# Even and odd rows kept apart in the block transforms, with other work between their steps

## Chip, cores and metric

The kernel runs on one core of a Trainium2 chip. The metric is the device time of one execution in microseconds (us). Before the change it was 556.54 us, the median of 3 runs from 553.25 to 558.03. An execution that takes over 1.5% longer than the fastest one of its kernel counts as slow.

## The reference

```python
def reference(A_q, A_k, A_v, A_shift_k, A_ssm_k, A_ssm_D, B_x, B_w1, B_w3, B_w2, c, w_mod):
    def _A_ref(q, k, v, shift_k, ssm_k, ssm_D):          # S = 2048 rows, D = 576 columns
        k_shift = ...            # causal convolution of k with 4 taps per column
        kv = k_shift * v
        # causal convolution over the 2048 rows, column by column, written with FFTs of length 2*S
        y_f = rfft(pad(kv)) * rfft(pad(ssm_k))
        y = irfft(y_f)[:S].astype(bfloat16) + kv * ssm_D
        return q * y
    x = A_q
    sa, ca, ga, sb, cb, gb = (silu(c) @ w_mod).reshape(...)
    h = layernorm(x) * (1 + ca) + sa
    x = x + ga * _A_ref(h, A_k, A_v, A_shift_k, A_ssm_k, A_ssm_D)
    h = layernorm(x) * (1 + cb) + sb
    return x + gb * ((silu(h @ B_w1) * (h @ B_w3)) @ B_w2)      # F = 4608 hidden columns
```

(Inputs are bfloat16.)

## The kernel before

The 2048 rows are cut into 8 blocks of 256. Each block of the signal `kv` and of the filter is transformed by matmuls with a matrix of sines and cosines. Products of the spectra X and V of different blocks are summed up in `z` by VectorE, and one inverse transform gives a block of the result. Two blocks make a row block of 512 rows for the feed-forward part; row block 3 has no convolution beside it. While TensorE works through the feed-forward part of row block r (the up projections, `stream`, then the down projection, `down`), the convolution of the next two blocks is fed in between in small steps: a step that is a generator yields its estimated VectorE time, and a negative yield means "let that much other work come first".

```python
def forward(self, basis, rhs, dst):                  # one transform: 4 outputs
    for e in range(2):
        for cs in range(2):
            ps = self.ps()                           # one of four accumulators
            for cc in range(2):                      # row parity: both are summed in PSUM
                for h in range(2):
                    nc.tensor.matmul(ps[:, h, 0:H], basis[:, cc, cs, e, :],
                                     rhs[:, cc, h * H:(h + 1) * H],
                                     start=(cc == 0), stop=(cc == 1))
            nc.scalar.copy(dst(e, cs)..., ps[:, :, 0:H])
            yield 0.4

def ln_scales(self, ssum, ssq, name):                # six small GpSimd operations on 128x2
    e.tensor_single_scalar(mean[:], ssum[:], -1.0 / D, op=ALU.mult)      # "l1m"
    e.tensor_scalar(var[:], ssq[:], 1.0 / D, EPS, op0=ALU.mult, op1=ALU.add)
    e.tensor_mul(rstd[:], mean[:], mean[:])
    e.tensor_sub(var[:], var[:], rstd[:])
    e.tensor_tensor(rstd[:], var[:], self.neghalf[:, 0:n], op=ALU.pow)
    e.tensor_mul(nmr[:], mean[:], rstd[:])                               # "l1n"

def gate_rows(self, s):                              # waits for l1n, in ScalarE's queue
    for i in range(2):
        self.nc.scalar.activation(hg[:, i, :], x1[:, i, :], ACT.Identity, bias=..., scale=...)

def conv(self, s0):                                  # blocks s0 and s1 = s0 + 1; cut
    def filters():
        yield from self.k_rows(s0);  yield -4.0
        yield from self.w_spectrum(s0);  yield -3.0
        yield from self.v_block(s0)
        yield from self.k_rows(s1);  yield -4.0
        yield from self.w_spectrum(s1)
    yield from self.mix(filters(), old())            # old(): products with kept spectra
    self.gate_stats(s0)
    yield from self.kv_rows(s0)                      # shift convolution
    yield from self.v_block(s1)
    self.gate_rows(s0)
    yield from self.x_spectrum(s0)                   # the signal's transform
    yield from self.pair(X0, self.V[s0], s0)
    ...
    yield from self.gate(s1)
    yield from self.pair(self.X[s1], V0, s1)
    yield from self.outcome(s1)                      # inverse, residual, second layernorm, transposes
```

(Cuts are marked by dots.) In `stream`, ScalarE empties an accumulator twice (`sg` = silu of the gate, `u` = copy of the up projection) and VectorE multiplies the two into `h`. `hg` are a block's rows after the first layernorm, `h2row` those after the second; the six operations of `ln_scales` make the scale and offset for either one (`l1...` and `l2...`). PSUM holds the accumulators `ps` that the matmuls write.

## Time and profile before

| | before |
|---|---|
| median of 4 runs | 555.5 us |
| span of the trace | 551.6 us |
| TensorE / VectorE / ScalarE / GpSimd busy | 519.7 / 317.1 / 302.2 / 47.0 us |
| TensorE idle | 31.9 us |

In the lines of the profile PE is TensorE, PEld its weight loads, DVE VectorE, ACT ScalarE, POOL GpSimd and SP the engine that issues transfers; `L414` is line 414 of that kernel; the granted clock is the share of TensorE's full clock that it was given. The reading of this profile stands in the prediction below. One line that the prediction did not look at became important. It is from the groups of instructions of the kernel before: engine, operation, output and inputs, count, busy us, mean ns, then the idle time before the group.

```profile
L414 POOL TENSOR_SCALAR l1m<-l1s 128x2 f32<-128x2 f32 x7 | 7.6, 1086 | 243.9 <-ACT junk L399 243.9
```

The timeline of GpSimd shows the longest of these seven and the statistics operation after it; start, duration, engine, line:

```profile
357.97 3.38 POOL L414 TENSOR_SCALAR l1m<-l1s 128x2 f32<-128x2 f32 x1 [63.30 <-ACT junk L399]
361.44 0.20 POOL L416 TENSOR_TENSOR l1r<-l1m 128x2 f32<-128x2 f32 x1
```

An operation on 128 x 2 elements normally takes about 0.20 us (0.72 us for the power) in this trace, as in the second line. This one took 3.38 us, and the mean of its group is 1.09 us. Little hung on it: ScalarE waited 0.5 us in all for such results at `hg` in blocks 1 to 7.

### The profile page before, as it was taken

What the parts mean: (1) busy time and instruction counts of PE and PEld (TensorE: products, weight loads), DVE (VectorE), ACT (ScalarE), POOL (GpSimd) and SP (SyncE); (2) the same over time, 40 slices, a digit from 0 to 9 for tenths busy, and PEclk for the clock granted to TensorE, in tenths of its full rate; (3) what the DMA queues carried; (4) which work ended last, traced back from release to release, by engine and by line L of the source; (5) the groups of instructions that cost most, each with busy time, mean ns of one, the idle gap of its engine ahead of it and who ended that gap; (6) DMA issues with size and microseconds to landing.
All of it is one profiled execution on the core that took longest, in us unless ns stands there. A gap on an engine that the chain in (4) does not pass through costs nothing.

```text
span 551.6 us, 9038 instructions
## 1 busy us (share of the span) xinstructions
PE 519.7 (94%) x3495; PEld 303.8 (55%) x3495; DVE 317.1 (57%) x489; ACT 302.2 (55%) x637; POOL 47.0 (9%) x111
## 2 busy tenths in 40 slices
PE   6978899998989999999998999989999999999996
PEld 3655665455757534434576644344478744444775
DVE  8989366796980286693983259979442111222011
ACT  6567697859532457749815165675956054554100
POOL 4321100203020000001001000030201000000000
PEclk9979999999998999999999999999999999999999
DMA  8945789998995686975997679654264545442452
GB/s 264 337 120 172 226 276 312 350 359 283 312 337 169 201 284 217 320 239 177 298 324 231 176 241 354 201 165 157 87 177 125 152 159 162 150 122 73 106 152 86
DMA packets 103214, 119.29 MB, mean 216 GB/s; under 512 B 5187, under 2 KB 93316, under 8 KB 103172
## 3 DMA queue, kind: packets, MB, share of 16 engines
q1 hardware_dynamic: 103150, 118.72, 68.4%
q8 instruction: 27, 0.44, 0.3%
q14 instruction: 15, 0.12, 0.1%
q10 hardware_dynamic: 22, 0.01, 0.0%
HBM read 104.84 MB, written 13.86 MB: 215 GB/s over the span
## 4 chain that ended last, share of the span: by engine, by line
PE 54%; DVE 18%; ACT 12%; DMA 9%; issue 4%; POOL 3%; SPq 1%; DVEq 0%; ACTq 0%
PE ps L821 25%; PE ps L875 20%; DMA wst<-in_B_w_dram 5%; DVE p L378 4%; ACT junk L399 4%; PE ps L828 4%; DVE z L380 3%; PE ps L286 3%; DMA X<-Xd 2%; DVE h L838 2%; ACT h2row L511 2%; DVE kvt L305 1%; DVE kv L306 1%; ACT sg L835 1%; ACT hg L454 1%
## 5 line engine op out<-in xcount | busy, mean ns | idle before, releaser
L821 PE MATMUL ps<-h2T,wst 128*128 128x512 bf16 (+1 forms) x1344 | 268.0, 349 | 6.1 <-DMA wst<-in_B_w_dram 4.9
L821 PEld LDWEIGHTS <-wst 128*128 128x128 bf16 x1344 | 125.8, 98 | 131.1 <-issue 20.8
L835 ACT ACTIVATE sg<-ps 128x512 bf16<-128x512 f32 (+1 forms) x168 | 91.7, 546 | 148.6 <-PE ps L828 98.3
L875 PE MATMUL ps<-w2t,h 128*128 128x288 bf16 x1152 | 145.3, 288 | 2.4 <-DMA w2t<-in_B_w_dram 2.4
L875 PEld LDWEIGHTS <-h 128*128 128x128 bf16 x1152 | 113.0, 98 | 32.3 <-DMA w2t<-in_B_w_dram 3.0
L838 DVE TENSOR_TENSOR h<-sg,u 128x512 bf16<-128x512 bf16 (+1 forms) x168 | 63.8, 384 | 106.6 <-ACT u L837 106.5
L837 ACT CAST u<-ps 128x512 bf16<-128x512 f32 (+1 forms) x168 | 89.2, 531 | 0.8 <-DVE h L838 0.8
L886 DVE TENSOR_TENSOR og<-ps,gbrow 128x288 bf16<-128x288 f32 x32 | 13.1, 451 | 83.5 <-PE ps L875 83.5
L378 DVE TENSOR_TENSOR p<-X,V 128x3456 bf16<-128x3456 bf16 x28 | 54.7, 1953 | 5.1 <-DMA X<-Xd 4.9
L380 DVE TENSOR_TENSOR z<-z,p 128x3456 bf16<-128x3456 bf16 x28 | 54.7, 1952 | 0.1
L399 ACT ACTIVATE junk<-x 128x576 bf16<-128x576 bf16 x58 | 40.2, 692 | 13.8 <-DVE x L499 13.3
L828 PE MATMUL ps<-h2T,wst 64*128 64x512 bf16 (+1 forms) x336 | 45.2, 350 | 0.8 <-ACT X L289 0.5
L414 POOL TENSOR_SCALAR l1m<-l1s 128x2 f32<-128x2 f32 x7 | 7.6, 1086 | 243.9 <-ACT junk L399 243.9
L828 PEld LDWEIGHTS <-wst 64*128 64x128 bf16 x336 | 10.6, 94 | 30.4 <-issue 27.4
L286 PE MATMUL ps<-kv,Fb 128*128 128x288 bf16 x128 | 19.0, 286 | 4.1 <-ACT u L837 2.3
L686 ACT CAST y<-ps 128x576 bf16<-128x576 f32 x14 | 8.9, 644 | 22.1 <-PE ps L483 22.1
L511 ACT ACTIVATE h2row<-x,l2n,l2r 128x576 bf16<-128x576 bf16 (+1 forms) x28 | 16.2, 676 | 8.0 <-POOL l2n L419 8.0
L305 DVE TENSOR_TENSOR kvt<-kh,shk 128x1152 bf16<-128x1152 bf16 x24 | 18.1, 753 | 1.8 <-DMA kh<-in_A_k_dram 1.7
L289 ACT CAST W<-ps 128x576 bf16<-128x576 f32 x32 | 18.9, 667 | 0.2 <-PE ps L286 0.2
L289 ACT CAST X<-ps 128x576 bf16<-128x576 f32 x32 | 18.9, 663 | 0.0
L286 PE MATMUL ps<-kT,Fk 128*128 128x288 bf16 x128 | 18.9, 296 | 0.0
L286 PEld LDWEIGHTS <-Fb 128*128 128x128 bf16 x128 | 11.8, 97 | 12.2 <-issue 6.7
(119 smaller groups left out, 327.3 us busy)
## 6 DMA issues: line engine op xcount, KB each, us to landing
wst<-in_B_w_dram SPq DMA_DIRECT2D x80, 512.0 KB, 5.5
w2t<-in_B_w_dram SPq DMA_DIRECT2D x72, 288.0 KB, 3.1
X<-Xd SPq DMA_DIRECT2D x12, 864.0 KB, 7.2
V<-Vd SPq DMA_DIRECT2D x10, 864.0 KB, 7.2
Vd<-V SPq DMA_DIRECT2D x7, 864.0 KB, 7.3
Xd<-X SPq DMA_DIRECT2D x6, 864.0 KB, 5.8
wst<-in_B_w_dram SPq DMA_DIRECT2D x80, 64.0 KB, 2.4
kh<-in_A_k_dram SPq DMA_DIRECT2D x7, 720.0 KB, 5.7
```

Of the source, the lines that this page charges most:

```text
L286: nc.tensor.matmul(ps[:, h, 0:H], basis[:, cc, cs, e, :], rhs[:, cc, h * H:(h + 1) * H], start=(cc == 0), stop=(cc == 1))
L289: nc.scalar.copy(dst(e, cs).rearrange("p (h d) -> p h d", h=2), ps[:, :, 0:H])
L378: nc.vector.tensor_mul(p[:], X[:], V[:])
L380: nc.vector.tensor_add(z[:], z[:], p[:])
L399: self.nc.scalar.activation(junk[:], src[:, i, :], func, accum_out=out[:, col:col + 1])
L511: self.nc.scalar.activation(row[:, cc, at:at + hi - lo], x1[:, cc, lo:hi], ACT.Identity, bias=b[:, cc:cc + 1], scale=r[:, cc:cc + 1])
L821: nc.tensor.matmul(gus[k][:, i, 0:t1 - t0], w[:, 5 * i + ct, cols], hT[:, ct, t0:t1], start=(first and ct == 0), stop=(not first and ct == 3))
L828: nc.tensor.matmul(gus[k][:, i, 0:t1 - t0], w[rows, 4, cols], hT[rows, 4, t0:t1], start=first, stop=not first)
L835: nc.scalar.activation(sg[:, 0:n], gus[k][:, 0, 0:n], ACT.Silu)
L837: nc.scalar.copy(u[:, 0:n], gus[k][:, 1, 0:n])
L838: nc.vector.tensor_mul(self.h3[:, fc * FC + fi, t0:t1], sg[:, 0:n], u[:, 0:n])
L875: nc.tensor.matmul(accs[t // 2][:, t % 2, 0:H], self.h3[:, f0 + f, t * P:(t + 1) * P], w[:, f, :], start=(f0 + f == 0), stop=(f0 + f == NF ...
```

## The change

The intent is to halve the transform matmuls of blocks 2 to 7. Even and odd rows (the two values of `cc`) are no longer summed in PSUM for each of two outputs; each is transformed once, and VectorE makes sum and difference. (In the filter's transform `cc` was the half of the block before; now it is the parity there too.) To keep the longer VectorE chain off TensorE's path, the order of the steps is changed too.

```diff
-CONV_US = (84.6, 91.6, 107.6)
+CONV_US = (86.0, 90.0, 100.0)
+SPLIT = 2                                  # blocks 0 and 1 keep forward()
+    def forward2(self, basis, rhs, both, odd, diff):
+        for cc, dst in ((0, both), (1, odd)):
+            for cs in range(2):
+                ps = self.ps()
+                for h in range(2):
+                    nc.tensor.matmul(ps[:, h, 0:H], basis[:, cc, cs], rhs[:, cc, h * H:(h + 1) * H],
+                                     start=True, stop=True)
+                nc.scalar.copy(dst[:, cs]..., ps[:, :, 0:H])
+                yield -1.9                  # other work between the parts
+        nc.vector.tensor_sub(diff, both, odd)
+        nc.vector.tensor_add(both, both, odd)
+        yield 1.5
@@ k_rows: the filter's columns are turned by parity
-                nc.tensor.transpose(pt[...], nat[:, ct, cc * P:(cc + 1) * P], self.ident[:])
+                nc.tensor.transpose(pt[...], nat[:, ct, cc:B:2], self.ident[:])
@@ real_parts, blocks 2 to 7: two more VectorE operations; inverse: 2 x 2 terms, not 4 x 2
+        nc.vector.tensor_add(z[:, 0:4:3, :], z[:, 1:3, :], z[:, 4:6, :])
+        nc.vector.tensor_sub(z[:, 1:3, :], z[:, 1:3, :], z[:, 4:6, :])
@@ conv: the order
-            yield from self.k_rows(s0)
-            yield -4.0
-            yield from self.w_spectrum(s0)
-            yield -3.0
+            if s0 == 2:
+                yield from self.filter_ahead(s0)
+                yield -3.0
             yield from self.v_block(s0)
 ...
-        yield from self.x_spectrum(s0)
-        yield from self.pair(X0, self.V[s0], s0)
 ...
+        yield from self.mix(self.x_spectrum(s0), beside())     # products between the parts
 ...
-        yield from self.outcome(s1)
+        yield from self.outcome(s1, self.mix(self.filter_ahead(s1 + 1)) if s1 + 1 < NBLK else ())
@@ stream: two half-width (256 columns) results share one accumulator and one product
-        items = [(job, fi) for job in jobs for fi in range(FC)]
+            m = RB // (job[2] - job[1])
+            items += [(job, fi, m) for fi in range(0, FC, m)]
@@ down: the last output half has four accumulators and sends each half row by itself
```

(Cut: the sine tables, the set-up, the rest of `conv`, `conv_second` and `stream`.)

## The prediction

"Such matmuls" are those with 288 columns: 128 of them took 15.68 us in the trace of the kernel before, 122.5 ns each, and by that the 144 matmuls are priced at 17.6 us. The 0.9 us for four more sine instructions is an estimate; in the traces two of them took 2.30 us before and six took 3.46 us after the change.

> **What bounds the kernel now.** I read the busy shares first, then the chain of waits, then TensorE's own waits, then the busy time by stage, and last the timeline of TensorE for the price of one matmul. The page:
>
> ```profile
> span 551.6 us, 9038 instructions
> PE 519.7 (94%) x3495; PEld 303.8 (55%) x3495; DVE 317.1 (57%) x489; ACT 302.2 (55%) x637; POOL 47.0 (9%) x111
> PE 54%; DVE 18%; ACT 12%; DMA 9%; issue 4%; POOL 3%; SPq 1%; DVEq 0%; ACTq 0%
> L286 PE MATMUL ps<-kv,Fb 128*128 128x288 bf16 x128 | 19.0, 286 | 4.1 <-ACT u L837 2.3
> L286 PE MATMUL ps<-kT,Fk 128*128 128x288 bf16 x128 | 18.9, 296 | 0.0
> L305 DVE TENSOR_TENSOR kvt<-kh,shk 128x1152 bf16<-128x1152 bf16 x24 | 18.1, 753 | 1.8 <-DMA kh<-in_A_k_dram 1.7
> ```
>
> TensorE is busy for 519.7 of 551.6 us, and no other engine reaches 60%. The chain puts only 54% on TensorE, but a chain names one of several paths of nearly equal length. Whether the others matter is told by the stages (busy us of each engine, with its count of instructions, the granted clock, the DMA share and GB/s):
>
> ```profile
> 31.80:73.60 41.80, 36.79 (x311) 25.50 (x309) 29.80 (x53) 32.35 (x86) 5.63 (x12) 0.97 0.57 182
> 73.60:139.20 65.60, 63.17 (x461) 37.49 (x461) 50.08 (x77) 51.06 (x123) 8.29 (x18) 1.00 0.94 314
> 139.20:183.70 44.50, 40.91 (x327) 31.42 (x325) 25.46 (x34) 14.55 (x32) 3.22 (x6) 0.96 0.82 257
> 183.70:272.00 88.30, 86.29 (x473) 37.98 (x471) 61.98 (x85) 63.16 (x126) 5.62 (x18) 1.00 0.79 254
> 272.00:312.80 40.80, 38.53 (x315) 30.15 (x314) 20.67 (x28) 11.21 (x24) 2.29 (x6) 1.00 0.80 241
> 312.80:402.00 89.20, 86.40 (x471) 38.16 (x469) 70.29 (x87) 60.70 (x119) 9.03 (x18) 1.00 0.62 201
> 402.00:440.00 38.00, 38.00 (x319) 30.27 (x318) 9.30 (x20) 13.97 (x30) 1.72 (x6) 1.00 0.57 155
> ```
>
> The first column is TensorE. I chose the cuts where the timeline changes between up projections and the down projection: 73.6 to 183.7 is row block 0 (the convolution of blocks 2 and 3 runs beside it), to 312.8 row block 1 (blocks 4 and 5), to 440 row block 2 (blocks 6 and 7). In these 366.4 us TensorE is busy for 353.3 us; VectorE for 237.8 us, 65%. So a matmul taken out here shortens the run nearly by its own time. TensorE's longest waits:
>
> ```profile
> PE ps L516 <- ACT h2row L511: 2.5, 2, 2.0
> PE ps L821 <- DMA wst<-in_B_w_dram: 1.3, 2, 1.0
> ```
>
> (73.6 to 183.7 us; total, times, longest.) They are small: about 2 us where the last block's normalized rows come late, about 1 us for weights.
>
> [...] a stretch of 128 such matmuls starts at 424.07 and the next work starts at 439.75, 15.68 us or 122.5 ns each. The 286 ns of the page's row is the length of one overlapped matmul, not its price. [...] after the 2.0 us gap near 164 us the clock fell to 0.70 for 165 to 170 us, and the next 128 matmuls took 17.35 us, not 15.68. [...] 753 ns for 1152 bf16 elements and 1953 ns for 3456 are about 0.52 ns an element and 150 ns fixed.
>
> **The change, part by part.**
>
> Removed from TensorE. A forward transform had 4 outputs x 2 row parities x 2 halves = 16 matmuls; kept apart, even and odd rows need 2 x 2 x 2 = 8, and sum and difference are made afterwards. There are 12 such transforms in blocks 2 to 7 (a filter and a signal each): 96 matmuls. The 6 inverses go from 16 to 8: 48 more. The instruction lists of the two programs agree: 288 TensorE instructions fewer, 144 matmuls with their weight loads. At 122.5 ns: **144 x 0.1225 = 17.6 us**. Blocks 0 and 1 keep the full transform.
>
> Added to VectorE. Two operations of 1152 elements per transform, 24 x 0.753 = 18.1 us; two more in each of 6 inverses, 12 x 0.753 = 9.0 us; 27.1 us in all. The half-width up projections of the first half of the rows are paired into one 512-wide bank: 48 products of 286 ns become 24 of 423 ns, 13.4 to 10.2 us, so VectorE gains 23.9 us, to about 341 us. On its own path this lies beside TensorE: in the three row blocks VectorE goes from 237.8 to about 265 us at most, in about 349 us, 76%.
>
> Removed from ScalarE. The same pairing turns 48 x (0.403 + 0.387) = 37.9 us into 24 x (0.603 + 0.588) = 28.6 us: 9.3 us less, beside TensorE. In the stage 31.8 to 73.6 us TensorE idles for 5.0 us, of which 2.7 are weights in flight; I give the pairing and the new order 1 us.
>
> Moved. The first filter's transform of the next pair of blocks goes under the down projection before it, and matmuls of a signal's transform are spread between products instead of standing in a row. In row blocks 1 and 2 TensorE waited 2.5 us for ScalarE before such transforms (1.7 for u, 0.8 for X); most should go: 1.5 us.
>
> Set-up. Six sine instructions instead of two, about 0.9 us more on ScalarE, but the first signal's transform waits for VectorE's kv chain (13.61 us), not for them: 0.
>
> Tail. The last output part uses four separate accumulators and sends each half row by itself. Before, two products and two sums follow the last matmul (547.27 to 548.52 us); after, one each: 0.8 us won. But these four accumulators are all the buffers there are, and the third and fourth wait until VectorE has emptied those of the first half: I estimate 0.8 us lost. Sum 0.
>
> Given back. After the last signal transform of block 3 VectorE must do two combining operations, the sums, a product and its addition, and four operations of the inverse; in the new order it has the next rows' shift convolution and the gate between these: 14 operations of 0.75 and 2 of 1.95 us, about 14.4 us, where TensorE has about 13 us of other work. Then comes the h2row chain that TensorE already waits for. I put 3 us of new waiting there with its clock loss, and 1 us for weights, since DMA is at 0.94 of its share from 73.6 to 139.2 us and the same bytes must come in about 4 us less.
>
> Sum: 17.6 + 1 + 1.5 - 3 - 1 = 16.1 us. From the median of 556.5: **540.4 us; I say 540**.
>
> **Rivals.** *VectorE becomes the bound.* For it: from 139.8 to 166.6 us it works with hardly a gap and TensorE waits for the row block's last rows; in row block 2 it is at 70.3 of 89.2 us. Against it: its additions come where TensorE has other matmuls in front, and it ends row block 2 with only 9.3 us in the last 38. If in each row block half of its addition reached TensorE, 12 us would come back: about 550 us, within 2%. *DMA takes over in row block 0.* For it: the share of 0.94 and 314 GB/s, with 350 and 359 in two slices. Against: row blocks 1 and 2 move 254 and 201 GB/s, so only block 0's own gain, about 5 us, is at stake: 545 us. *Waits vanish too.* TensorE idles 13.1 us in the three blocks and 5.0 before them; if the spreading took away half, the time would be 532 us.
>
> **Range and chances.** The 17.6 us rest on a count and a measured price; open is what returns as waiting, 0 to 10 us, and 2 us of spread between runs (553.25 to 558.03). So 533 to 547 us. Faster by over 2% means below 545.4 us: 0.86. Within 2%: 0.13. Slower by over 2% would need more than 28 us of new stalls: 0.01.
>
> **What would show it.** Right: TensorE's busy time near 502 us and 144 matmuls fewer; VectorE near 341 and ScalarE near 293 us; row blocks 1 and 2 some 5 to 8 us shorter each; transposes still about 56 ns apart; last product to end about 0.8 us shorter. Wrong: idle TensorE before the inverse or before the transposes of h2row in the down projection of row block 0, with VectorE named; longer waits for wst; granted clock below 0.95 after such gaps; a gap at the start of the last output half.

## The result

The changed kernel took 534.18 us (median of 4 runs, 532.99 to 534.99), against 555.5 us (553.25 to 558.03). The ratio is 0.9613, with a 95% interval of 0.9564 to 0.9663: faster. Ratios here are the mean time of one kernel's fast runs over that of the other's fast runs of the same rounds, so they are not quite the ratio of the medians quoted. The time lies within the predicted range, near its low end.

From the page of the changed kernel:

```profile
span 533.2 us, 8728 instructions
PE 500.0 (94%) x3351; PEld 293.7 (55%) x3351; DVE 339.7 (64%) x502; ACT 298.4 (56%) x593; POOL 62.1 (12%) x113
PE 60%; DVE 21%; ACT 9%; DMA 4%; POOL 3%; issue 2%; SPq 0%; ACTq 0%; DVEq 0%
L450 POOL TENSOR_SCALAR l1m<-l1s 128x2 f32<-128x2 f32 x7 | 19.3, 2753 | 223.0 <-ACT junk L435 223.0
```

TensorE lost 19.7 us of busy time and 144 matmuls, and its idle time is nearly the same, 33.2 for 31.9 us: nearly all that was taken out shortened the run. VectorE gained 22.6 us. The last line is a surprise: the GpSimd operation above now takes 2.75 us on average.

The stages of the changed kernel, cut at the same places in the work (columns: stretch, length, busy us of TensorE, its weight loads, VectorE, ScalarE and GpSimd with counts of instructions, granted clock, DMA share, GB/s):

```profile
32.30:76.00 43.70, 37.55 (x311) 27.65 (x309) 29.92 (x43) 29.32 (x62) 6.45 (x12) 0.91 0.54 172
76.00:138.20 62.20, 56.22 (x414) 33.55 (x414) 46.71 (x65) 43.26 (x87) 4.61 (x7) 1.00 0.92 297
138.20:182.20 44.00, 41.71 (x342) 32.66 (x341) 32.61 (x45) 24.80 (x49) 11.56 (x18) 0.96 0.91 299
182.20:262.70 80.50, 79.68 (x415) 33.04 (x414) 68.93 (x93) 58.45 (x119) 14.80 (x18) 1.00 0.79 263
262.70:302.90 40.20, 38.66 (x326) 30.83 (x325) 23.64 (x31) 15.75 (x31) 1.86 (x6) 1.00 0.94 299
302.90:384.00 81.10, 78.84 (x405) 32.48 (x403) 72.85 (x90) 53.25 (x108) 9.68 (x14) 1.00 0.66 215
384.00:421.90 37.90, 37.47 (x316) 30.02 (x316) 15.78 (x26) 17.75 (x36) 3.04 (x11) 1.00 0.56 152
```

| stage | before | after |
|---|---|---|
| up to the start of row block 0 | 73.6 | 76.0 |
| row block 0 | 110.1 | 106.2 |
| row block 1 | 129.1 | 120.6 |
| row block 2 | 126.9 | 119.1 |
| rest | 111.9 | 111.3 |

(The table is cut at the first up projection of each row block, the windows above and in the prediction at rounded places: their sums differ from it by up to 0.3 us.)

Row blocks 1 and 2 give 16.3 us, row block 0 gives 3.9, and the stage before it takes 2.4 back. The set-up accounts for 0.4 of that (the first up projection starts at 34.17, not 33.75 us). The other 2 us come with one new stall. The timeline of the changed kernel around it, on VectorE, GpSimd, ScalarE and TensorE:

```profile
44.90 1.95 DVE L409 TENSOR_TENSOR z<-X,V 128x3456 bf16<-128x3456 bf16 x1
45.24 1.67 POOL L455 TENSOR_TENSOR l1n<-l1m,l1r 128x2 f32<-128x2 f32 x1
46.94 1.62 ACT L490 ACTIVATE hg<-x,l1n,l1r 128x576 bf16<-128x576 bf16 x2 [2.41 <-POOL l1n L455]
49.57 0.65 PE L299 MATMUL ps<-kv,Fb 128*128 128x288 bf16 x4 [3.27 <-ACT u L894]
```

The bracket is the idle time of the engine before the instruction, and what ended it. The sixth statistics operation took 1.67 us, not 0.2, and ended at 46.91 us, just after VectorE's product of two inputs (46.85; e8 comes back to this). ScalarE's queue waited 2.41 us for it at `hg`; behind `hg` in that queue were the copies that empty the accumulators, and TensorE stood still for 3.27 us. The granted clock of the stage fell to 0.91.

TensorE's longest waits in row block 0 of the changed kernel, from 76 to 182.2 us (total, times, longest):

```profile
PE ps L874 <- DMA wst<-in_B_w_dram: 5.3, 5, 1.7
PE ps L561 <- ACT h2row L556: 2.3, 1, 2.3
```

The waits for weights rose from 1.3 to 5.3 us; the wait for `h2row` did not grow (2.5 before).

### The profile page after: what moved, and what is told of

It is laid out like the page before. It is cut to its first block, busy times and chain, and to the rows that moved or that the text cites. A ratio compares the mean times of both kernels' runs of the same rounds, so it can differ in the third digit from the quotient of the medians.

```text
span 533.2 us, 8728 instructions
## 1 busy us (share of the span) xinstructions
PE 500.0 (94%) x3351; PEld 293.7 (55%) x3351; DVE 339.7 (64%) x502; ACT 298.4 (56%) x593; POOL 62.1 (12%) x113
## 4 chain that ended last, share of the span: by engine, by line
PE 60%; DVE 21%; ACT 9%; DMA 4%; POOL 3%; issue 2%; SPq 0%; ACTq 0%; DVEq 0%
PE ps L874 27%; PE ps L937 24%; DVE p L414 5%; DVE z L416 5%; PE ps L885 4%; DVE h L896 3%; ACT junk L435 3%; DMA wst<-in_B_w_dram 2%; DMA w2t<-in_B_w_dram 1%; PE ps L313 1%; DVE kv L335 1%; ACT sg L892 1%; PE ps L299 1%; PE ps L529 1%; ACT h2row L556 1%
## 5 line engine op out<-in xcount | busy, mean ns | idle before, releaser
L874 PEld LDWEIGHTS <-wst 128*128 128x128 bf16 x1344 | 128.1, 98 | 131.9 <-issue 20.6
L892 ACT ACTIVATE sg<-ps 128x512 bf16<-128x512 f32 x144 | 86.5, 601 | 130.7 <-PE ps L885 84.6
L896 DVE TENSOR_TENSOR h<-sg,u 128x512 bf16<-128x512 bf16 x144 | 60.2, 420 | 93.3 <-ACT u L894 93.2
L894 ACT CAST u<-ps 128x512 bf16<-128x512 f32 x144 | 84.3, 586 | 0.0
L450 POOL TENSOR_SCALAR l1m<-l1s 128x2 f32<-128x2 f32 x7 | 19.3, 2753 | 223.0 <-ACT junk L435 223.0
L885 PE MATMUL ps<-h2T,wst 64*128 64x512 bf16 (+1 forms) x336 | 42.3, 350 | 0.0
L589 ACT ACTIVATE h2T<-ps,sbcol,cbcol 128x256 bf16<-128x256 bf16 x35 | 16.7, 569 | 10.1 <-PE ps L561 10.1
L335 DVE TENSOR_TENSOR kv<-kv,kvt 128x1152 bf16<-128x1152 bf16 x24 | 18.1, 753 | 0.4
L409 DVE TENSOR_TENSOR z<-X,V 128x3456 bf16<-128x3456 bf16 x7 | 13.5, 1954 | 4.8 <-DMA V<-Vd 4.7
L315 ACT CAST X<-ps 128x576 bf16<-128x576 f32 x24 | 15.5, 652 | 0.8 <-PE ps L313 0.8
L490 ACT ACTIVATE hg<-x,l1n,l1r 128x576 bf16<-128x576 bf16 x14 | 11.5, 881 | 2.4 <-POOL l1n L455 2.4
```

Of the source, the lines that this page charges most:

```text
L335: nc.vector.tensor_add(kv[:], kv[:], tmp[:])
L874: nc.tensor.matmul(gus[k][:, i, a * n:(a + 1) * n], w[:, 5 * i + ct, (fi + a) * P:(fi + a + 1) * P], hT[:, ct, t0:t1], start=(first and ct ...
L885: nc.tensor.matmul(gus[k][:, i, a * n:(a + 1) * n], w[rows, 4, (fi + a) * P:(fi + a + 1) * P], hT[rows, 4, t0:t1], start=(first and a == 0 ...
L892: nc.scalar.activation(sg[:], gus[k][:, 0, :], ACT.Silu)
L894: nc.scalar.copy(u[:], gus[k][:, 1, :])
L896: nc.vector.tensor_mul(self.h3[:, f:f + m, t0:t1], sg[:].rearrange("p (a t) -> p a t", a=m), u[:].rearrange("p (a t) -> p a t", a=m))
```

## The experiments

Twelve kernels were run. Each was timed against the kernel before on its own chip, so that figures are compared by their ratios; 0.01 of the ratio is 5.5 us. The changed kernel itself ("after", from here on) was not run again.

### e2_matmuls_back: what the matmuls alone are worth

```diff
-                for h in range(2):                       # forward2
+                for h in (0, 1, 0, 1):
-            terms = [(3 * cc, 1, cc), (3 * cc, 0, 3 - cc)]      # inverse
+            terms = [(3 * cc, 1, cc), (3 * cc, 0, 3 - cc)] * 2
+        n = 4 if s < SPLIT else 2                        # and start/stop by i % n
```

> The changed kernel in which each matmul of the split transforms and inverses is done twice, the second overwriting the first (right result): 144 matmuls more, VectorE and ScalarE unchanged. Theory: + 144 x 0.1225 = 17.6 us, about 552 us, TensorE busy about 517 us. Rival (the gain came from elsewhere, TensorE had slack): below 542 us.

Every split matmul is done twice, so the 144 are back and all else is as in after. Measured: 545.7 us (545.16 to 547.85), ratio 0.9848 (0.98 to 0.9895). Against after that is 11.5 us by the medians, 13 by the ratios (0.0235 x 555), not 17.6: between the theory and its rival. The trace says where the rest is: row block 0 ended only 2.1 us later than in after, although about 7 us of matmuls had been added up to there; the other row blocks took 5.0 and 3.2 us more. What follows: with the new order in place, a removed matmul passes on about two thirds to three quarters of its time. The remaining 8.4 us of the gain (0.0152 x 555) are there with the old count of matmuls: order, pairing and tail together (by e5 below, the pairing adds nothing to it).

### e4_split_old_order: the same matmuls gone, in the old order

The conv, conv_second, stream and down of the kernel before, with the split transforms in them (shown against after):

```diff
-                yield -1.9                  # forward2
+                yield 0.4
-        yield from self.outcome(s1, self.mix(self.filter_ahead(s1 + 1)) if s1 + 1 < NBLK else ())
+        yield from self.outcome(s1)         # and the old conv(), conv_second(), stream(), down()
-CONV_US = (86.0, 90.0, 100.0)
+CONV_US = (93.6, 100.6, 116.6)
```

> The kernel before with the split transforms alone: old order of steps, old unpaired half-width projections, old tail; pacing constants raised by the 9 us of added steps. Theory: nearly all of the gain is here, 555.5 - 17.6 and up to 5 us of new waits behind the longer VectorE chains: 538 to 544 us. Rival (the split gains only together with the new order): 548 us or more.

Measured: 553.47 us (551.26 to 558.23), ratio 0.9996 (0.9918 to 1.0073). **The split alone gains nothing that these runs can tell** (the interval leaves about 4 us either way), as the rival had said. The old order was tried with one setting of its pacing constants. TensorE's busy time fell to 503.3 us, as it should, but its idle time rose to 48.3 us in a span of 551.6, the same as before. From the page of this run:

```profile
L313 PE MATMUL ps<-kv,Fb 128*128 128x288 bf16 x48 | 9.3, 298 | 12.3 <-ACT X L315 10.2
```

TensorE stood for 12.3 us before the matmuls of the signals' transforms, 10.2 of it for accumulators that ScalarE had yet to copy to X. The largest of these stalls, on the timeline of the same run:

```profile
352.31 8.03 POOL L450 TENSOR_SCALAR l1m<-l1s 128x2 f32<-128x2 f32 x1 [62.82 <-ACT junk L435]
...
359.83 0.42 DVE L882 TENSOR_TENSOR h<-sg,u 128x512 bf16<-128x512 bf16 x1
...
362.15 1.62 ACT L490 ACTIVATE hg<-x,l1n,l1r 128x576 bf16<-128x576 bf16 x2 [5.14 <-POOL l1n L455]
...
364.35 0.64 PE L313 MATMUL ps<-kv,Fb 128*128 128x288 bf16 x2 [6.89 <-ACT X L315]
```

The statistics operation lasted from 352.31 to 360.34. VectorE's instructions followed each other without a gap until 360.25. Then the five other statistics took their usual time (0.19 or 0.20 us, 0.72 for the power), ScalarE's `hg` could start, the copies behind it came, and TensorE went on after 6.89 us. Row block 1 was 5.4 us shorter than before, row block 2 was 5.3 us longer.

### e1_new_order_full: the new order with the full transforms

```diff
-SPLIT = 2
+SPLIT = 8
```

> The changed kernel with the full transforms in all blocks (the 144 matmuls are back, the 36 added VectorE operations are gone; new order, pairing and tail stay). Theory (TensorE's count of matmuls sets the time): 534.2 + 17.6 = about 552 us, 548 to 555. Rival (the new order, not the split, gave the gain): about 537 us, within 1% of the changed kernel.

Measured: 558.19 us (557.32 to 562.33), ratio 1.008 (1.0023 to 1.0138): missed. The run is not the clean counterpart of e4, because the full `forward` yields 0.4 and not -1.9 between its parts, so they are issued in a row. That makes it useful in another way. It has the same number of matmuls as e2 (x3495 weight loads in both pages) and 21.5 us less VectorE work, and on the same chip it was slower than e2 by 0.0232 of the ratio, 13 us. What e2 has is the spreading of the parts (and the split's data flow). One statistics operation lasted longest of all here; behind it ScalarE waited 7.84 us at `h2row` and TensorE 3.74 us:

```profile
119.79 16.82 POOL L450 TENSOR_SCALAR l1m<-l1s 128x2 f32<-128x2 f32 x1 [33.41 <-ACT junk L435]
```

### e12_signal_in_a_row and e11_no_filter_ahead: the two moves, one at a time

```diff
# e12
-    def forward2(self, basis, rhs, both, odd, diff):
+    def forward2(self, basis, rhs, both, odd, diff, step=-1.9):
-                yield -1.9
+                yield step                  # x_spectrum passes 0.4
# e11
-            if s0 == 2:
-                yield from self.filter_ahead(s0)
-                yield -3.0
+            yield from self.filter_ahead(s0)
+            yield -3.0
-        yield from self.outcome(s1, self.mix(self.filter_ahead(s1 + 1)) if s1 + 1 < NBLK else ())
+        yield from self.outcome(s1)
```

> The changed kernel with the four parts of each split signal transform issued in a row and the products after them, as in the old order; the filters keep their places. Theory (TensorE and ScalarE wait on each other's accumulators when four parts come at once): 3 to 8 us more, 537 to 542 us. Rival (the filter's new place is all that counts): within 2 us of 534.

> The changed kernel with the first filter's transform of blocks 4 and 6 back at the start of their own row block, not under the down projection before. Theory (VectorE stands nearly idle under the down projections of row blocks 1 and 2 and is full in the first part of the next; work moved there is what makes room): 5 to 10 us more, 539 to 545 us. Rival (the interleaving of the signal transforms makes the room): within 3 us of 534.

e12 took 547.05 us (543.52 to 549.38), ratio 0.987 (0.9817 to 0.9924): 13 to 14 us more than after, where the theory had said 3 to 8. TensorE's waits from 130 us on, in this run:

```profile
PE ps L561 <- ACT h2row L556: 5.3, 4, 2.9
PE ps L313 <- ACT u L894: 4.2, 3, 2.2
PE ps L874 <- ACT u L894: 2.6, 3, 1.8
```

In after the same three are 2.8, 0.2 and 0.7 us. A signal's transform in a row needs accumulators faster than ScalarE gives them back (`ps L313`, the matmuls of these transforms). The longest statistics operation was shorter here than in after (4.84 against 8.60 us), but ScalarE's waits for the statistics of the second layernorm, at `h2row`, rose from 7.4 to 13.3 us, so that a part of this loss may come by way of GpSimd.

e11 took 555.13 us (551.88 to 557.11), ratio 1.0016 (0.9971 to 1.0061): 21 us more than after, as much as the whole gain, where the theory had said 5 to 10. The down projection of row block 1, 40.2 us in after, took 52.6 us; of the rest, 6.0 us more went by in row block 0. The stage of that down projection, then its longest stops on the timeline, on VectorE, ScalarE and TensorE:

```profile
271.20:323.80 52.60, 41.96 (x317) 31.67 (x317) 39.77 (x44) 17.82 (x36) 10.94 (x11) 0.90 0.74 247
```

```profile
274.43 1.96 DVE L409 TENSOR_TENSOR z<-X,V 128x3456 bf16<-128x3456 bf16 x1 [6.29 <-DMA X<-Xd]
```

```profile
313.96 2.28 ACT L556 ACTIVATE h2row<-x,l2n,l2r 128x576 bf16<-128x576 bf16 x4 [9.19 <-POOL l2n L455]
314.89 0.39 PE L561 MATMUL ps<-ident,h2row 128*128 128x128 bf16 x2 [5.31 <-ACT h2row L556]
```

VectorE's queue stood for 6.29 us at a product of the next pair of blocks, whose X had not landed yet, while work for `h2row` was queued behind it. Then came GpSimd: the six statistics that `h2row` needs lasted from 304.06 to 313.93, 9.87 us, while VectorE was busy for 15.55 of the 16 us from 298 to 314. TensorE had nothing to do before the transposes of `h2row`. So the moved transform does more than fill a gap: in its absence the scheduler brings the next pair's first product forward into the chain that ends this row block. How much of the 21 us the late order, the stretched statistics and the unfilled gap each have was not separated.

### e3_vector_double and e13_vector_less: does VectorE's work lie beside TensorE?

```diff
# e3: done three times instead of once, +36 operations, about +27 us of VectorE
+        for _ in range(3):
-        nc.vector.tensor_sub(diff, both, odd)
+            nc.vector.tensor_sub(diff, both, odd)
+        for _ in range(3):
-        nc.vector.tensor_add(z[:, 0:4:3, :], z[:, 1:3, :], z[:, 4:6, :])
+            nc.vector.tensor_add(z[:, 0:4:3, :], z[:, 1:3, :], z[:, 4:6, :])
# e13: 18 operations left out, about -13.5 us; the values are wrong on purpose
-        nc.vector.tensor_add(both, both, odd)
-        nc.vector.tensor_sub(z[:, 1:3, :], z[:, 1:3, :], z[:, 4:6, :])
```

> The changed kernel with the 36 added VectorE operations done twice (36 operations of 1152 elements more, 27 us of VectorE; right result). Theory (they lie beside TensorE): at most 4 us more, 534 to 538 us. Rival (VectorE is now the bound, or as near it as TensorE): half to all of it, 547 to 561 us.

> The changed kernel without 18 of its 36 added VectorE operations (the sum of each transform and the last difference of each inverse are left out; the result is wrong on purpose), 13.5 us of VectorE less, the same matmuls. Theory now (VectorE's queue is on the path in row blocks 0 and 2; doubling 27 us cost 20.6 us): 4 to 10 us less, 524 to 530 us. Rival (doubling only crossed a threshold; as it stands the changed kernel is bound by TensorE alone): within 2 us of 534.

e3 took 554.79 us (553.25 to 557.59), ratio 1.001 (0.9956 to 1.0064): 20.6 us more than after by the medians, 0.76 us for each us of VectorE added. My theory had said at most 4; the rival was right. Two paths are visible. TensorE waited 5.9 us before inverse transforms for VectorE's own result `z`, and 9.8 us before the transposes of `h2row`. The longest of the latter on the timeline, first GpSimd, then TensorE:

```profile
133.50 14.61 POOL L451 TENSOR_SCALAR l1m<-l1s 128x2 f32<-128x2 f32 x1 [46.63 <-ACT junk L436]
```

```profile
154.20 0.71 PE L563 MATMUL ps<-ident,h2row 128*128 128x128 bf16 x5 [6.63 <-ACT h2row L558]
```

Between the two, the other statistics ran until 153.24 us, and ScalarE began `h2row` behind them at 153.28.

e13 took 531.55 us (530.63 to 533.46), ratio 0.9601 (0.9567 to 0.9634). Taking 13.5 us from VectorE gave 2.6 us by the medians and 0.7 by the ratios, within the spread: less than the theory's 4 to 10, near the rival. (The values of e13 are wrong, though the comparison with the reference, with its tolerance, still passed.) So the changed kernel sits just below the point at which VectorE begins to set the time: less work there wins next to nothing, more costs three quarters of itself.

### e8_gap, e9_old_order_gap, e10_full_gap: do VectorE's products stretch the statistics, and does a gap cure it?

The theory was that GpSimd's statistics do not end while VectorE's instructions with two inputs follow each other without a gap. The traces so far fit it: the operations of 7.35 and 8.60 us in after and of 8.03 us in e4 ended 0.08 or 0.09 us after the last instruction of such a row (142.65 after 142.57, 248.74 after 248.65, 360.34 after 360.25). That an instruction with one input between them would let GpSimd go on was my guess; no trace had shown it. So each gated product got a copy of one element before it, on top of after (e8), of e4 (e9) and of e1 (e10). That is 144 copies, but 168 in e9, where the narrow products are not paired (its expectation below says 144):

```diff
+            nc.vector.tensor_copy(self.h3[:, f, t0:t0 + 1], sg[:, 0:1])
             nc.vector.tensor_mul(self.h3[:, f:f + m, t0:t1], sg[:]..., u[:]...)
```

> The changed kernel with one VectorE copy of a single element per partition (one SBUF input, overwritten by the product) ahead of each of the 144 gated products. New theory: GpSimd's statistics, normally 0.2 us each, cannot start while VectorE runs two-input operations back to back (7.4 and 8.6 us were seen), and a one-input instruction between lets them in: the longest statistics operation falls below 2.5 us. Time: [...] 530 to 537 us. Rival (those long GpSimd times come from a wait for their input, not from VectorE): the longest stays above 5 us.

> Run 4 (split transforms, old order) with the same 144 one-element copies. New theory: the 8.0 us GpSimd operation that held ScalarE, and with it TensorE for 6.9 us, falls below 2.5 us and the time to 542 to 548 us. Rival (the old order is slow for its VectorE chains alone): 551 us or more.

> Run 1 (full transforms in the new order) with the same 144 one-element copies. New theory: its 16.8 us GpSimd operation falls below 2.5 us and the time from 558 to 546 to 552 us, that is 534 plus the price of 144 matmuls. Rival (the new order without the split is slow for another reason): 556 us or more.

| run | time (range) | ratio (95%) | longest statistics operation | without the copies |
|---|---|---|---|---|
| e8 | 542.03 (539.8 to 547.34) | 0.9818 (0.9777 to 0.986) | 3.49 us | 8.60 (after) |
| e9 | 556.5 (555.8 to 557.28) | 1.0069 (1.0038 to 1.0101) | 3.77 us | 8.03 (e4) |
| e10 | 560.91 (560.24 to 561.67; without the slow run of 569.5) | 1.0156 (1.0111 to 1.0201) | 5.64 us | 16.82 (e1) |

The forecasts failed in all three: no longest operation fell below 2.5 us (in e10 it stayed above the 5 us of e8's rival), and no time came into its range; e9 and e10 took what their rivals had said. Yet the timeline of e8 fits the theory, operation by operation. Four operations of GpSimd and three of VectorE's copies in it, in order of time:

```profile
244.13 1.57 POOL L450 TENSOR_SCALAR l1m<-l1s 128x2 f32<-128x2 f32 x1 [25.85 <-ACT junk L435]
245.54 0.14 DVE L896 COPY h<-sg 128x1 bf16<-128x1 bf16 x1
245.78 2.82 POOL L452 TENSOR_TENSOR l1r<-l1m 128x2 f32<-128x2 f32 x1
248.47 0.15 DVE L896 COPY h<-sg 128x1 bf16<-128x1 bf16 x1
248.57 1.76 POOL L451 TENSOR_SCALAR l1v<-l1q 128x2 f32<-128x2 f32 x1
250.21 0.14 DVE L896 COPY h<-sg 128x1 bf16<-128x1 bf16 x1
250.42 2.18 POOL L453 TENSOR_TENSOR l1v<-l1v,l1r 128x2 f32<-128x2 f32 x1
```

The operations end at 245.70, 248.60 and 250.33, each 0.12 to 0.16 us after a copy has begun. VectorE made no pause at these copies: each began 0.08 us or so before the recorded end of the product ahead of it, as VectorE's other instructions do there. So a pause of VectorE is not what let GpSimd go on there; the copies fit. At each of these copies one operation ended, and the next one ended only at the next copy (the fourth at 252.60, with a copy at 252.47). From the start of `l1m` to the end of `l1n` it takes 9.6 us, against 10.5 in after (240.14 to 250.68). The copies came as seldom as the gated products: in e8 2.93, 1.74 and 2.26 us lie between these four. In e9 the stall of TensorE was still 6.27 us, with operations of 2.80, 2.29 and 2.18 us in place of the one of 8.03. Besides, a copy of one element took 0.152 us, 144 of them 21.8 us of VectorE, more than I had allowed for; in e3 27 us more of VectorE cost 20.6 us. My estimate was careless: the prediction's own two durations, 753 ns for 1152 elements and 1953 ns for 3456, leave about 150 ns that do not depend on the length. The loss of these runs is therefore no evidence against the theory; what the long statistics cost in the time stays unmeasured. A kernel with the statistics on another engine, which would measure it, was not run.

### e5_no_pair and e6_gate_later: the pairing and the stall at 49.6 us

```diff
# e5: stream() of the kernel before in the changed kernel
-            m = RB // (job[2] - job[1])
-            items += [(job, fi, m) for fi in range(0, FC, m)]
+        items = [(job, fi) for job in jobs for fi in range(FC)]
# e6: conv_second(); ScalarE's hg comes after the transform
-        self.gate_rows(1)
         yield from self.pair(self.X[0], self.V[1], 1)
         yield from self.x_spectrum(1)
         self.mod_piece(5)
+        self.gate_rows(1)
```

> The changed kernel with the half-width projections unpaired as before (48 narrow instead of 24 full gated products; 3.2 us of VectorE and 9.3 us of ScalarE more, in row block 0). Theory (VectorE is on the path there): 2 to 5 us more, 536 to 539 us. Rival (pairing delays the first statistics of block 1 and so costs what it wins): within 1.5 us of 534, or less.

> The changed kernel with the two normalizing ScalarE instructions of block 1 issued after the four copies of that block's signal transform, not before. In the changed kernel they waited 2.4 us for GpSimd at the head of ScalarE's queue, and TensorE stood 3.3 us for a free accumulator behind them. Theory: that wait goes, with its clock loss: 3 to 5 us less, about 530 us. Rival (another wait takes its place, the stage waits for weights anyway): within 1 us of the changed kernel.

e5 took 529.66 us (528.67 to 532.66), ratio 0.9571 (0.9524 to 0.9618). The pairing was expected to win 2 to 5 us and did not: without it the time is 4.5 us shorter by the medians and 2.3 by the ratios. The ranges of the runs do not overlap with those of after, the intervals of the ratios do, and the two were not run in the same call, so the size stays open. The traces agree on the place: row block 0 ends at 176.9, not 182.2 us, and afterwards all stages are equal within 0.4 us. The stall of 3.27 us is not there. e5 has the lowest time of all kernels run.

e6 took 530.6 us (528.76 to 532.45), ratio 0.9599 (0.9569 to 0.9629). The stall is gone and row block 0 ends 2.3 us earlier in the trace. Against after that is 3.6 us by the medians, as the theory had said, but 0.8 us (0.14%) by the ratios, less than the interval can tell. The two edits together were not run.

## Why the prediction was right, and where its steps were not

The time was right, in the lower part of the range; the sum was near through steps that erred in opposite directions, and that is luck. By e2 the matmuls gave 11.5 to 13 us, for 17.6, and everything else together gave 8.4, for a forecast net loss of 1.5 (1 + 1.5 - 3 - 1).

**Counts and busy times held, but for ScalarE.** TensorE 500.0 for 502 us, VectorE 339.7 for 341; ScalarE 298.4 for 293, a fall of 3.8 us where 9.3 were forecast; 144 matmuls fewer. Row blocks 1 and 2 became 8.5 and 7.8 us shorter, for 5 to 8. The transposes of every second column cost nothing more: ten of them start at 98.83 and the next work at 99.40 us, 57 ns each, as before the change (315.17 to 315.74).

**"144 x 0.1225 = 17.6 us" was mis-sized as a gain.** The price of one matmul is right, but that all of it reaches the end was assumed from TensorE's share of 94%. e2 measured 11.5 to 13 us, and in the old order e4 measured about 0.

**"Moved: 1.5 us" is the step that failed most.** I had valued the new order by the waits that it could remove from the kernel before. But those waits are small in the kernel before; with the split in the old order TensorE's idle time grew from 31.9 to 48.3 us, which ate all that was saved (e4). e2 shows 8.4 us of gain at the old count of matmuls, and e11 and e12 show that without one of the two moves 13 to 21 us are lost. The parts are not additive: the split in the old order gains nothing, either move undone loses most or all, and together they give 21 us.

**"On its own path this lies beside TensorE", and the rival "VectorE becomes the bound".** True only as the kernel stands, with nothing to spare: e13 shows 0.7 to 2.6 us from 13.5 us less, e3 shows 20.6 us from 27 more. A share of 76% did not tell this. The rival was judged by whether VectorE's own results come late. In after TensorE did not wait for `z` before an inverse in the three row blocks; in e3 it did, for 5.9 us. But VectorE's work also reached TensorE by a road that I had not looked for: the six GpSimd statistics of a layernorm. One of them lasted 7.35 us and another 8.60 us in after while VectorE's two-input instructions followed each other without a gap. (ScalarE's waits for the products `h`, which free its buffers, are no different: 15.1 us before, 15.0 in after; only e3 has more, 21.2.)

The timelines of after show the road: `l1m` lasts from 135.30 to 142.65.

```profile
135.30 7.35 POOL L450 TENSOR_SCALAR l1m<-l1s 128x2 f32<-128x2 f32 x1 [48.60 <-ACT junk L435]
141.83 0.74 DVE L334 TENSOR_TENSOR kvt<-kh,shk 128x1152 bf16<-128x1152 bf16 x1
142.74 0.20 POOL L452 TENSOR_TENSOR l1r<-l1m 128x2 f32<-128x2 f32 x1
145.04 0.76 DVE L331 TENSOR_TENSOR kv<-kh,shk 128x1152 bf16<-128x1152 bf16 x1 [2.47 <-PE ps L313]
```

VectorE's last instruction before its pause ends at 142.57, `l1m` ends 0.08 us later, and the next statistics take 0.20 us again while VectorE is idle. Here nothing waited for it: `hg` of this block started at 153.35 us without a wait for GpSimd. In e3 and e4 TensorE stood for over 6 us at the end of such a wait.

**"Pairing and the new order: 1 us" in the stage before row block 0** had the wrong sign: that stage became longer by 2.4 us with the set-up, its clock fell to 0.91, and in e5 and e6 the stall at 49.57 is gone and row block 0 ends earlier.

**"Given back: 3 us" and "1 us for weights".** The wait before the inverse and the longer wait for `h2row` did not come. Weights cost 4 us more instead of 1, in row block 0, where the share of the DMA was high already (0.94 in its first part). TensorE was busy 6.2 us less there (104.1 to 97.9), and 3.9 us of that reached the end, because other waits became 1.7 us shorter.

**The tail** was called 0.8 won and 0.8 lost. From the last matmul to the end it takes 3.9 us instead of 4.6, 0.6 or 0.7 us won; no gap appears at the start of the last output half, where 288 matmuls in a row took 35.48 us. The loss did not come; the tail alone was not run.

**The prediction's reading of the clock.** The gap of 2.0 us is one part of the pause: but for ten transposes TensorE had no work from 162.88 to 166.34 us. The 0.70 is a mean; from 167 to 170 us the clock was 0.5.

Open: how the losses of e1, e3, e11 and e12 divide between the long statistics and the changed order of the queues; what the new pacing constants do, which were changed with the order and never alone; and what e5 and e6 are worth against after in one call.

## What to carry to other kernels

When the busiest engine gets less to do, the work that kept it supplied has less time too (in e4 TensorE had 16.4 us less to do and was idle 16.4 us longer): value a reordering by the waits that will exist after the removal, not by those in the trace before it, and test the removal without the reordering. A share of 76% for a helper engine does not say that it has slack; doubling its added work on purpose does (27 us more cost 20.6 us in e3). Tiny operations in a chain on GpSimd, read by an engine that also empties accumulators, deserve a look at their durations whenever VectorE's stream becomes denser (an operation of 0.20 us lasted up to 8.60 us in after, 14.61 us in e3 and 16.82 us in e1).
